# The first expert as 128 early rows and 88 on halves of the array, the second in a fixed third place with its weights loaded in the attention

## The chip, the core and the metric

One core of one Trainium2 chip. The metric is the device time of one execution in microseconds (us); smaller is better. The engines are PE (matmuls; weight loads are recorded apart as PEld), DVE, ACT, POOL and SP. Each takes its instructions in order; SP issues direct transfers, POOL the indirect ones (gathers and scatters by a list of row numbers).

## What is computed

A gated linear recurrence over 4 batches x 8 heads x 768 positions of width 48, and on its output, 3072 tokens of width 384, a mixture of 16 experts chosen in two steps (4 groups of 4). All is float32. Cut to what matters:

```python
for t in range(S):                                   # attention
    state = alpha[:, :, t, :, None] * state + einsum('bhd,bhe->bhde', k[:, :, t], v[:, :, t])
    y[:, :, t] = einsum('bhd,bhde->bhe', q[:, :, t], state)
x = y.transpose(0, 2, 1, 3).reshape(3072, 384)
g = argmax(x @ w_group, 1)                           # mixture
for each group g, expert e (argmax of xg @ w_expert[g]):
    h = maximum(x[tokens] @ w1[g, e], 0)             # 384 -> 1024
    out[tokens] = (g_w * e_w)[:, None] * (h @ w2[g, e])   # 1024 -> 384
```

With the inputs that the reference draws, the experts get 213, 184, 202, 191, 211, 196, 184, 200, 180, 158, 195, 181, 168, 194, 205 and 210 tokens. Of the first 2048 tokens (16 tiles) 131 go to expert 0, of the first 1536 (12 tiles) 96.

## The kernel before, in words

**Attention.** The sequence is cut into 24 chunks (tiles) of 128 tokens, and the recurrence of a chunk is done with matmuls: scores (`scores`, L428), masked, then outputs (`outputs`, L506), what the state adds (`from_before`, L494), the new state (`gains`, L463), and rows and logits (`to_rows`, L527). `outputs` and `gains` write their heads in turn to the lower and upper 64 partitions, so their matmuls use one half of the array's columns at a time. All of this is a list of pieces of work with an engine, a planned duration (`takes`), a time after which others may use the result (`serves`), an action and what it needs; `in_turns` (L35) plans them in order of planned time and due time, and the instructions are emitted in that order, which then is each engine's order. Pieces named below: `OUTn` outputs of chunk n; `LGn` logits; `PAg`, `PBg`, `WTg`, `CNTg`, `PLg` the choice of experts, weights and places for a group g of chunks (L800); `Xt` the scatter of tile t's rows into their expert's slots in `slots_d` (POOL, L625). On SP and on PE the order is that in which the code adds the pieces.

**Slots.** Each expert has slots in DRAM, and a token's place is its number within the expert. `fill` writes blanks first. Inputs q, k and alpha are loaded into buffers that are at the same time the two buffers of expert weights (`homes`, L304; the pool of `w1`, `w2` has two buffers each): a unit's input sits in the first weight buffer when (u + 1) % 3 is 0, in the second when it is 1. Unit 8 is the last in the first, unit 9 the last in the second.

**Early rows.** The first expert's first 96 slots (`EARLY`) are full once the first 12 tiles (`EARLY_T`) are scattered. `LW` (L792) loads its weights into the first buffer when unit 8 has left it, `ER` (L793) reads the 96 rows when `X11` has landed, `ET` turns them on DVE (L649), and the end of the attention on PE is interleaved with their hidden layer: `E0` to `E3`, each two f-blocks (`early`, L875), with relus `A0` to `A3` on ACT, then `RP` (L953), two thirds of their result. The last third (L1189) follows after the attention's PSUM pools have given way to a pool of 7 banks (L969).

**Mixture.** `jobs` (L1131): job 0 the 96 early rows of expert 0, job 1 its slots 96 to 223, then 15 jobs, the other experts in order of their number of tokens, each rank with a fixed number of rows `cap(r)` (L154): 216, 213, ... 180, then 171 and 168. `by_number` (L1097, DVE) sorts; SP reads each job's expert from the result. Per job: `fetch_rows` (SP, up to three jobs ahead), `columns` (DVE transposes of 32x32), `hidden` (24 matmuls and 4 relus), `result` (24 matmuls and 2 copies), `deliver_quarters` (DVE, then one indirect scatter per 32 rows on POOL). Rows are the moving operand; the weights, 128x128 at a time, are loaded for each matmul. The weights of job j + 2 are loaded once job j has left its buffer (L1200); those of job 2 are loaded after its rows are fetched (L1193). Tokens beyond a job's rows would be done in a loop at the end whose number of turns is read from the data.

The two parts that do the matmuls, as they are before:

```python
nc.tensor.matmul(z[:, k * n:(k + 1) * n], lhsT=w1[:, dc, f * P:(f + 1) * P],
                 rhs=xt[:, dc, 0:n], start=(dc == 0), stop=(dc == DC - 1))
```

## Time and profile before

| | |
|---|---|
| median of three runs | 397.62 us (394.83 to 399.1) |
| the profiled execution | 390.5 us |
| its span | 388.8 us, TensorE clock granted 0.992 |
| PE busy | 374.7 us, 96% of the span, 3366 instructions |
| weight loads busy | 356.6 us, 92% |
| POOL, DVE, ACT busy | 195.3, 162.4, 139.3 us |
| DMA | 95.22 MB, mean 245 GB/s |
| first matmul of job 1, of job 2 | 129.73, 141.47 us |

How to read it: the page gives each engine's busy time, the span in 40 slices (9.72 us each) with the DMA rate in each, the chain of work that ended last, followed back from the end, and groups of instructions. The timeline lists instructions in order of start, runs of the same kind merged into one line, with the idle time before and what ended it. An f32 matmul is two instructions in these counts.

### The profile page before, as it was taken

The page shows a single profiled execution, that of the slowest core. Times are in us where ns is not written, and L with a number is a line of the kernel's source. Part 1 is how long each engine was busy: PE and PEld are TensorE (multiplying, and loading weights), DVE is VectorE, ACT ScalarE, POOL GpSimd, SP SyncE. Part 2 cuts the span into 40 slices and gives each one's busy share as a digit, 9 for nine tenths or more (in the row PEclk, how much of TensorE's full clock was granted, in tenths as well). Part 3 has the DMA queues.
Part 4 walks back from the last instruction along what each step waited for, and adds up shares of the span by engine and source line. Part 5 has one row for each costly group of instructions (what it writes and reads, how often), then busy time and mean ns, then how long its engine had stood idle before and what let it go on. Part 6 is the DMA issues. An engine that isn't in the chain of part 4 may idle for free.

```text
span 388.8 us, 8864 instructions
## 1 busy us (share of the span) xinstructions
PE 374.7 (96%) x3366; PEld 356.6 (92%) x3366; DVE 162.4 (42%) x420; ACT 139.3 (36%) x379; POOL 195.3 (50%) x240
## 2 busy tenths in 40 slices
PE   8999999999999899999999999999999999999990
PEld 3888998898989899999999999999999999999990
DVE  7999998899868220207322020220201202202200
ACT  5989899596762211111121121211212112112110
POOL 5988886888746321244261633526336235144341
PEclk9999999999999999999999999999999999999996
DMA  8999999994313799986585866768668777665000
GB/s 284 380 410 412 413 358 352 410 417 172 100 64 128 154 328 346 333 244 219 175 255 218 276 220 207 224 227 282 227 201 257 269 245 240 249 250 182 16 22 27
DMA packets 32411, 95.22 MB, mean 245 GB/s; under 512 B 18175, under 2 KB 18454, under 8 KB 27888
## 3 DMA queue, kind: packets, MB, share of 16 engines
q1 hardware_dynamic: 27552, 85.10, 63.5%
q0 software_dynamic: 4816, 9.55, 7.3%
q8 instruction: 27, 0.44, 0.5%
q14 instruction: 16, 0.13, 0.1%
HBM read 79.47 MB, written 15.56 MB: 244 GB/s over the span
## 4 chain that ended last, share of the span: by engine, by line
PE 69%; DMA 18%; issue 5%; POOL 4%; SPq 1%; DVE 1%; POOLq 0%; ACT 0%; DVEq 0%; ACTq 0%
PE bank L237 29%; PE bank L248 29%; DMA slots_d<-blank 7%; DMA qka<-in_qka_dram 5%; DMA w<-in_qka_dram 3%; PE zo L506 3%; PE zs L428 3%; PE bank L527 2%; DMA out_dram<-yq,dst_q 2%; POOL out_dram L1023 1%; DMA v<-in_v_dram 1%; PE zo L494 1%; SPq L320 1%; POOL slots_d L625 1%; PE bank L446 1%
## 5 line engine op out<-in xcount | busy, mean ns | idle before, releaser
L1023 POOL DMA_INDIRECT out_dram<-yq,dst_q x99 | 96.4, 974 | 153.2 <-DVE yq L1019 121.3
L237 PE MATMUL bank<-xt_e,w 128*128 128x128 f32 (+15 forms) x768 | 126.5, 325 | 1.4 <-DVE dst_q L1045 0.8
L248 PE MATMUL bank<-hT,w 128*128 128x128 f32 (+15 forms) x768 | 126.3, 324 | 0.0
L237 PEld LDWEIGHTS bank<-xt_e,w 128*128 128x128 f32 x768 | 124.1, 190 | 1.7 <-PE bank L248 0.9
L248 PEld LDWEIGHTS bank<-hT,w 128*128 128x128 f32 x768 | 124.1, 190 | 0.0
L1040 DVE CAST dst_q<-xq 128x7 int32<-128x7 f32 (+2 forms) x16 | 2.7, 168 | 168.8 <-DMA out_dram<-yq,dst_q 168.8
L239 ACT ACTIVATE hT<-bank 128x256 f32<-128x256 f32 (+15 forms) x64 | 31.3, 489 | 96.3 <-PE bank L237 96.3
L250 ACT COPY yT<-bank 128x256 f32<-128x256 f32 (+31 forms) x32 | 12.7, 398 | 109.0 <-PE bank L248 109.0
L625 POOL DMA_INDIRECT slots_d<-xr,place x24 | 24.1, 1002 | 10.6 <-issue 3.3
L506 PE MATMUL zo<-sm,v 128*48 128x128 f32 (+1 forms) x384 | 27.2, 280 | 1.0 <-POOL sm L437 1.0
L428 PE MATMUL zs<-qp,kp 48*128 48x128 f32 x384 | 28.2, 285 | 0.0
L527 PE MATMUL bank<-wr,yt 112*128 112x116 f32 x192 | 26.1, 279 | 0.5 <-ACT sm L856 0.5
L506 PEld LDWEIGHTS zo<-sm,v 128*48 128x48 f32 (+1 forms) x384 | 20.3, 129 | 6.5 <-POOL sm L437 2.4
L428 PEld LDWEIGHTS zs<-qp,kp 48*128 48x128 f32 x384 | 23.4, 187 | 2.6 <-DVE qp L414 0.8
L527 PEld LDWEIGHTS bank<-wr,yt 112*128 112x128 f32 x192 | 23.3, 191 | 0.9 <-ACT sm L856 0.7
L405 ACT ACTIVATE w<-w,whole 112x128 f32<-112x128 f32 x60 | 19.8, 402 | 2.0 <-DMA w<-in_qka_dram 2.0
L378 DVE TENSOR_TENSOR_SCAN rev<-w,starts 112x387 f32<-112x387 f32 (+1 forms) x22 | 18.5, 869 | 3.4 <-DMA w<-in_qka_dram 3.4
L414 POOL TENSOR_TENSOR kp<-w,rev 112x384 f32<-112x384 f32 (+1 forms) x21 | 18.3, 886 | 2.2 <-DVE rev L378 2.0
L414 POOL TENSOR_TENSOR qp<-w,cq 112x384 f32<-112x384 f32 (+1 forms) x20 | 17.1, 862 | 4.4 <-ACT w L405 3.9
L433 DVE TENSOR_TENSOR sm<-zs,causal 128x512 f32<-128x512 f32 x28 | 18.3, 679 | 2.4 <-PE zs L428 2.2
L388 DVE TENSOR_TENSOR_SCAN cq<-w,starts 112x387 f32<-112x387 f32 (+1 forms) x22 | 19.1, 871 | 0.0
L1016 DVE STREAM_TRANSPOSE yq<-yT 128x672 f32<-128x672 f32 (+2 forms) x15 | 12.3, 818 | 15.5 <-ACT yT L250 15.4
(135 smaller groups left out, 340.6 us busy)
## 6 DMA issues: line engine op xcount, KB each, us to landing
w<-in_w_dram SPq DMA_DIRECT2D x32, 1536.0 KB, 7.1
w<-in_qka_dram SPq DMA_DIRECT2D x16, 578.0 KB, 10.4
slots_d<-blank SPq DMA_DIRECT2D x4, 1372.0 KB, 19.1
qka<-in_qka_dram SPq DMA_DIRECT2D x8, 578.0 KB, 12.7
v<-in_v_dram SPq DMA_DIRECT2D x3, 1152.0 KB, 15.8
xq<-slots_d SPq DMA_DIRECT2D x32, 85.8 KB, 7.6
qka<-in_qka_dram SPq DMA_DIRECT2D x6, 385.5 KB, 6.3
xq<-slots_d SPq DMA_DIRECT2D x28, 73.5 KB, 6.3
```

The source lines that it names most:

```text
L237: nc.tensor.matmul(z[:, k * n:(k + 1) * n], lhsT=w1[:, dc, f * P:(f + 1) * P], rhs=xt[:, dc, 0:n], start=(dc == 0), stop=(dc == DC - 1))
L239: return lambda: nc.scalar.activation(out=hT[:, f0:f0 + 2, 0:n], in_=z[:, 0:2 * n].rearrange("p (f t) -> p f t", f=2), func=AF.Relu)
L248: nc.tensor.matmul(z[:, i * n:(i + 1) * n], lhsT=w2[:, f, dc * P:(dc + 1) * P], rhs=hT[:, f, 0:n], start=(f == 0), stop=(f == FC - 1))
L378: nc.vector.tensor_tensor_scan(out=part_of("rev", u, i, A1).rearrange("r c s -> r (c s)")[:, ::-1], data0=a[:, W:0:-1], data1=one_col.to_b ...
L388: nc.vector.tensor_tensor_scan(out=cq, data0=a[:, 0:n * A1], data1=starts[0:R, 0:n * A1], initial=1.0, op0=ALU.mult, op1=ALU.min)
L405: nc.scalar.activation(out=q[:, j, :], in_=q[:, j, :], func=AF.Copy, scale=ready["whole", u][:, i * g + j // k, c:c + 1])
L414: engine.tensor_tensor(out=part_of(kind, u, i, P), in0=of, in1=by[:, :, 1:A1], op=ALU.mult)
L428: nc.tensor.matmul(z[i][:, p, :], lhsT=kp[r, p, c, :], rhs=qp[r, p, c, :], start=True, stop=True)
L506: nc.tensor.matmul(of(z, p)[o], lhsT=vs[b][:, bc, h * D:h * D + o.stop - o.start], rhs=sm[:, i, p, :], start=(p < 2 and bc == 0), stop=Tru ...
L527: nc.tensor.matmul(z[:, at:at + W], lhsT=yt[:, p, :], rhs=wr[:, p, :], start=(p == 0), stop=(p % 2 == 1), skip_group_check=True)
L625: dma = nc.gpsimd.indirect_dma_start(out=slots_by[cs.start + c], out_offset=bass.IndirectOffsetOnAxis(ap=it["to"][:, c:c + 1], axis=0), in ...
L1023: nc.gpsimd.indirect_dma_start(out=out_by.popleft().rearrange("n (j w) -> (n j) w", j=4), out_offset=bass.IndirectOffsetOnAxis(ap=dst[:, b ...
```

## The change

What it does, part by part:

- The early rows become 128, read after tile 15 (`EARLY_T` = 16); no group of tiles ends at 16, so the step that raises the count (L614) is no longer reached. All three thirds of their result are in `RP`, in one bank; the last third after the attention is gone.
- Job 1 is the remaining 88 slots of the first expert, which now has 216 in all. Where a job has fewer than 128 rows, `sides` gives two halves, and each 128x128 product is done as two of 64 columns, written to the lower and upper 64 partitions of the same bank, one after the other.
- The second expert is job 2, with 188 rows (`FIXED_CAPS`), whatever its number of tokens. The ranks are 14: 216, 213, ... 183, then 174 and 171.
- Its weights are loaded by `LX`, in SP's order behind `ER`, into the second buffer, when unit 9 has left it. The load at the start of the mixture is gone, and the sort is emitted before the fetch of job 3's rows, not job 2's.
- `blank`, which also holds the early rows' hidden layer, grows to 1024 columns.

```diff
--- before.py
+++ after.py
@@ -148,7 +148,8 @@
     G = Eg = 4
     NL = G + NE
     CAP = 224
-    FIXED, EARLY, EARLY_T, BLK = 1, 96, (B // 2) * NC, 112
+    FIXED, EARLY, EARLY_T, BLK = 2, P, (B // 2) * NC + 4, 112
+    FIXED_CAPS = [CAP - 8, CAP - 36]
     NS = NE - FIXED
 
     def cap(r):
@@ -159,6 +160,7 @@
     XW = 4 * QW
     NB = CAP // 32
     heads = [slice(0, D), slice(64, 64 + D)]
+    halves = [slice(0, 64), slice(64, P)]
 
     cp = ctx.enter_context(tc.tile_pool(name="consts", bufs=1))
     wp = ctx.enter_context(tc.tile_pool(name="weights", bufs=2))
@@ -207,7 +209,7 @@
     wr = cp.tile([R, HP, D2 + NL], F32, name="wr")
 
     picked = cp.tile([P, NT, NE], BF16, name="picked")
-    blank = cp.tile([P, 2 * XW], F32, name="blank")
+    blank = cp.tile([P, max(2 * XW, FC * EARLY)], F32, name="blank")
     seen = cp.tile([P, NT + 1, NE], F32, name="seen")
 
     xr = cp.tile([P, NT, XW], F32, name="xr")
@@ -230,23 +232,31 @@
         weights[i] = (w1, w2)
         return dma.ins
 
-    def hidden_part(z, w1, xt, hT, f0, n, halves=(0, 1)):
-        for k in halves:
-            f = f0 + k
+    def sides(n):
+
+        return [slice(0, P)] if n >= P else halves
+
+    def hidden_part(z, w1, xt, hT, f0, n, of=(0, 1)):
+        for k in of:
+            at = (f0 + k) * P
             for dc in range(DC):
-                nc.tensor.matmul(z[:, k * n:(k + 1) * n], lhsT=w1[:, dc, f * P:(f + 1) * P],
-                                 rhs=xt[:, dc, 0:n], start=(dc == 0), stop=(dc == DC - 1))
+                for x in sides(n):
+                    nc.tensor.matmul(z[x, k * n:(k + 1) * n],
+                                     lhsT=w1[:, dc, at + x.start:at + x.stop],
+                                     rhs=xt[:, dc, 0:n], start=(dc == 0), stop=(dc == DC - 1))
         return lambda: nc.scalar.activation(
             out=hT[:, f0:f0 + 2, 0:n], in_=z[:, 0:2 * n].rearrange("p (f t) -> p f t", f=2),
             func=AF.Relu)
 
-    def result_part(z, w2, hT, yT, d0, n):
-        k = min(2, DC - d0)
+    def result_part(z, w2, hT, yT, d0, n, k=2):
+        k = min(k, DC - d0)
         for i in range(k):
-            dc = d0 + i
+            at = (d0 + i) * P
             for f in range(FC):
-                nc.tensor.matmul(z[:, i * n:(i + 1) * n], lhsT=w2[:, f, dc * P:(dc + 1) * P],
-                                 rhs=hT[:, f, 0:n], start=(f == 0), stop=(f == FC - 1))
+                for x in sides(n):
+                    nc.tensor.matmul(z[x, i * n:(i + 1) * n],
+                                     lhsT=w2[:, f, at + x.start:at + x.stop],
+                                     rhs=hT[:, f, 0:n], start=(f == 0), stop=(f == FC - 1))
         return lambda: nc.scalar.copy(out=yT[:, d0:d0 + k, 0:n],
                                       in_=z[:, 0:k * n].rearrange("p (c t) -> p c t", c=k))
 
@@ -289,7 +299,7 @@
         for t in state:
             nc.scalar.copy(out=t.rearrange("r p e -> r (p e)"),
                            in_=zeros[0:R, 0:1].to_broadcast([R, HP * 64]))
-        nc.scalar.copy(out=blank, in_=zeros[:, 0:1].to_broadcast([P, 2 * XW]))
+        nc.scalar.copy(out=blank[:, 0:2 * XW], in_=zeros[:, 0:1].to_broadcast([P, 2 * XW]))
         nc.scalar.copy(out=quarters[:, :, :, QW - 1], in_=quarter_f)
 
         NU = len(units)
@@ -611,7 +621,7 @@
                 old, new = seen[:, cs.start, :], seen[:, cs.stop, :]
                 nc.vector.tensor_tensor(out=new, in0=rk[:, C, :], in1=old, op=ALU.add)
                 if cs.stop == EARLY_T:
-                    nc.vector.tensor_scalar(out=new[:, 0:FIXED], in0=new[:, 0:FIXED],
+                    nc.vector.tensor_scalar(out=new[:, 0:1], in0=new[:, 0:1],
                                             scalar1=float(EARLY), scalar2=None, op0=ALU.max)
                 rk = rk[:, 0:C]
                 nc.vector.tensor_tensor(out=rk, in0=rk, in1=old[:, None, :]
@@ -654,7 +664,7 @@
             in_turn(
                 out=slots_d.rearrange("(e n) w -> e n w", e=NE)[e:e + n, 0:CAP, :].rearrange(
                     "e (p t) w -> p e (t w)", t=2),
-                in_=blank[0:CAP // 2, None, :].to_broadcast([CAP // 2, n, 2 * XW]))
+                in_=blank[0:CAP // 2, None, 0:2 * XW].to_broadcast([CAP // 2, n, 2 * XW]))
 
         later = {}
 
@@ -664,8 +674,8 @@
             later["desc_f"] = iota("desc_f", [P, 4], [[-1, 4]], base=4)
             nc.gpsimd.iota(out=seen[:, 0, :], pattern=[[N, NE]], base=0, channel_multiplier=0,
                            allow_small_or_imprecise_dtypes=True)
-            nc.gpsimd.memset(blank.rearrange("p (k w) -> p k w", w=QW)[:, :, QW - 1:QW],
-                             float(4 * N))
+            nc.gpsimd.memset(blank[:, 0:2 * XW].rearrange("p (k w) -> p k w", w=QW)
+                             [:, :, QW - 1:QW], float(4 * N))
 
 
 
@@ -791,6 +801,8 @@
         lent = max(u for u in range(NU) if (u + 1) % 3 == 0)
         queued("LW", 7.5, 9.5, lambda: load_weights(0, 0, in_turn), each("KP", lent) + each("QP", lent))
         queued("ER", 2.0, 5.0, read_early, [f"X{EARLY_T - 1}"])
+        lent = max(u for u in range(NU) if (u + 1) % 3 == 1)
+        queued("LX", 7.5, 9.5, lambda: load_weights(2, 1, in_turn), each("KP", lent) + each("QP", lent))
         add("CONST", POOL, 0.6, 0.7, constants, each("QP", 0))
         add("DESC", DVE, 0.13, 0.25,
              lambda: nc.vector.tensor_copy(out=desc, in_=later["desc_f"]), ["CONST"])
@@ -950,10 +962,10 @@
                 count(g)
         early(2)
         early(3)
-        on_array("RP", 3.0, 3.2, lambda: hold.update(RP=result_part(
-            bank(), weights[0][1], early_hT, early_xt, 0, EARLY)), ["A0", "A1", "A2", ("A3", 0.6)],
-            readers=["AR"])
-        add("AR", ACT, 0.4, 0.55, lambda: hold["RP"](), ["RP"])
+        on_array("RP", 5.2, 5.4, lambda: hold.update(RP=result_part(
+            bank(), weights[0][1], early_hT, early_xt, 0, EARLY, DC)),
+            ["A0", "A1", "A2", ("A3", 0.6)], readers=["AR"])
+        add("AR", ACT, 0.5, 0.65, lambda: hold["RP"](), ["RP"])
 
         all_ = {name: Work(e, takes, serves, emit, (), due)
                 for name, (e, takes, serves, emit, _, _, due) in works.items()}
@@ -1116,7 +1128,8 @@
         with nc.allow_low_precision("whole numbers below 2**24"):
             nc.vector.tensor_reduce(out=order, in_=sq, axis=AX.X, op=ALU.add)
         excess, ceiling = (rp.tile([P, NE], F32, name=k) for k in ("excess", "ceiling"))
-        nc.vector.memset(ceiling[:, 0:FIXED], float(CAP))
+        for e, n in enumerate(FIXED_CAPS):
+            nc.vector.memset(ceiling[:, e:e + 1], float(n))
         nc.vector.tensor_scalar(out=ceiling[:, FIXED:NE], in0=rank, scalar1=float(cap(1) - cap(0)),
                                 scalar2=float(cap(0)), op0=ALU.mult, op1=ALU.add)
         drop = cap(1) - cap(0) + cap(NS - 3) - cap(NS - 2)
@@ -1128,7 +1141,8 @@
         nc.vector.tensor_tensor(out=ceiling, in0=ceiling, in1=seen[:, 0, :], op=ALU.add)
         return order, excess, ceiling
 
-    jobs = [dict(e=0, n=EARLY, rows=early_rows), dict(e=0, c0=EARLY, n=CAP - EARLY)]
+    jobs = [dict(e=0, n=EARLY, rows=early_rows), dict(e=0, c0=EARLY, n=FIXED_CAPS[0] - EARLY),
+            dict(e=1, c0=0, n=FIXED_CAPS[1])]
     jobs += [dict(r=r, c0=0, n=cap(r)) for r in range(NS)]
     for job in jobs:
         job["nb"] = -(-job["n"] // 32)
@@ -1176,23 +1190,17 @@
     AHEAD = 3
     for j, job in enumerate(jobs):
         for k in range(1 if j == 0 else j + AHEAD, j + AHEAD + 1):
-            if k == 2:
+            if k == 3:
                 order, excess, ceiling = by_number()
             if k < len(jobs):
-                dma = fetch_rows(jobs[k])
-                if k == 2:
-                    fetched = dma.ins.name
+                fetch_rows(jobs[k])
         width = job["n"]
-        w1, w2 = weights[0] if j < 2 * FIXED else weights.pop(j)
+        w1, w2 = weights[0] if j < 2 else weights.pop(j)
         dst = destined(job)
         if j == 0:
-            result_part(bank(), w2, early_hT, early_xt, 2, EARLY)()
             last = (job, early_xt, dst)
             for t in results:
                 nc.gpsimd.memset(t, 0.0)
-            tc.add_manual_dep(load_weights(2, expert(jobs[2])), fetched, mybir.DependencyInfo(
-                mybir.DependencyClass.NoSync, mybir.DependencyReason.SCHED_ONLY),
-                reason="the rows go ahead of the weights")
             xt = columns(jobs[1])
             continue
         hT = hidden(w1, xt, width, {2: [deliver_last]})
```

## The prediction

> **What bounds the kernel.** I read the page first: PE is busy 96% of the span, and the chain that ended last is PE for 69%.
>
> ```profile
> PE 69%; DMA 18%; issue 5%; POOL 4%; SPq 1%; DVE 1%; POOLq 0%; ACT 0%; DVEq 0%; ACTq 0%
> ```
>
> Then the chain in order of time (start, length, what). From 141.47 us it is matmuls alone, job after job; its last two lines are the job with 171 rows:
>
> ```profile
> 350.74 6.96 PE bank L237 x48
> 357.70 6.97 PE bank L248 x48
> ```
>
> A job is 48 matmuls; an f32 matmul is two instructions, hence 96. 13.93 us / 96 = 145 ns, which is (171 + 3) / 1.2. The same holds for 180 rows (7.32 + 7.32 us) and 213 (8.64 + 8.64). So a job of n rows costs 0.08 us x (n + 3), and one row more anywhere costs 0.08 us.
>
> Next PE's timeline where attention hands over (start, length, operation, shapes, instructions, idle before and releaser):
>
> ```profile
> 116.19 0.91 PE L237 MATMUL zs<-early_xt,w 128*128 128x96 f32 x6
> 116.94 0.18 PE L601 MATMUL bank<-picked,before 128*128 128x32 bf16 x1
> 120.21 2.90 PE L237 MATMUL bank<-early_xt,w 128*128 128x96 f32 x24
> 122.95 3.74 PE L248 MATMUL bank<-blank,w 128*128 128x96 f32 x32
> 127.09 2.02 PE L248 MATMUL bank<-blank,w 128*128 128x96 f32 x16 [0.41 <-ACT early_xt L250]
> 129.73 5.62 PE L237 MATMUL bank<-xt_e,w 128*128 128x128 f32 x48 [0.61 <-DVE dst_q L1040]
> 135.19 5.52 PE L248 MATMUL bank<-hT,w 128*128 128x128 f32 x48
> 141.47 0.79 PE L237 MATMUL bank<-xt_e,w 128*128 128x216 f32 x3 [0.76 <-DVE dst_q L1045]
> ```
>
> The reader is to see two things. With 96 rows, 24 instructions take 122.95 - 120.21 = 2.74 us, 114 ns each; with 128 rows, 48 take 135.19 - 129.73 = 5.46 us, 114 ns each. So 96 and 128 rows cost the same: a floor holds both, about 11.0 us a job. And PE idles only 0.41, 0.61 and 0.76 us. The last idle time is put down to dst_q, but the matmul reads only xt_e, which was done at 132.84, and the weights; these were issued at 132.41 (SP's timeline below), so they end this wait.
>
> The same timeline has matmuls on halves of the columns. Outputs (L506: 64 or 48 columns, 128 moving rows) and gains (L463: 64 or 48 columns, 48 rows) alternate sides:
>
> ```profile
> 110.84 1.09 PE L506 MATMUL zo<-sm,v 128*48 128x128 f32 x16
> 111.75 0.64 PE L463 MATMUL bank<-v,kt 128*48 128x48 f32 x16
> 112.31 1.16 PE L428 MATMUL zs<-qp,kp 48*128 48x128 f32 x16
> ```
>
> From start to start 16 instructions take 0.91 us (57 ns) and 0.56 us (35 ns). On the whole array 131 / 1.2 = 109 ns each would be needed for L506, so two halves run at once.
>
> Last, the queues and DVE around the early rows:
>
> ```profile
> 98.11 1.01 POOL L625 DMA_INDIRECT slots_d<-xr,place  x1 [0.15 <-DVE starts L591]
> 106.46 0.97 POOL L625 DMA_INDIRECT slots_d<-xr,place  x1 [1.79 <-DVE lg L533]
> 100.93 2.73 SPq L320 DMA_DIRECT2D early_rows<-slots_d  x4
> 132.41 0.35 SPq L226 DMA_DIRECT2D w<-in_w_dram  x1
> 106.21 0.47 DVE L649 STREAM_TRANSPOSE early_xt<-early_rows 128x288 f32<-128x288 f32 x1
> 115.08 0.19 DVE L533 TENSOR_REDUCE lg<-bank 128x20 f32<-128x40 f32 x1
> 116.67 0.19 DVE L577 TENSOR_TENSOR picked<-oh,starts 128x32 bf16<-128x32 f32 x1
> ```
>
> Counting scatters back from the last (X23, 122.46), 98.11 is X11 and 106.46 is X15. The early rows' transposition began 8.1 us after X11's start.
>
> **What the Trainium skill says.** TensorE: Matmul & The Clock Gate, section LDWEIGHTS: a weight load takes its columns / 1.2 ns, 106.7 for 128. The trace agrees: loads of 128, 64 and 48 columns last 190, 137 and 123 ns, 0.83 ns a column, and the floor of 114 ns is 107 plus some. The same page, Part 3, says that loads overlap matmuls in flight only when the row group differs, which halves of columns do not. TensorEngine Tiling (Array Packing), Key Properties, says that different tiles load and multiply in parallel, and that changing the mode drains the engine. L463 sides with the second page: its 16 loads, 896 columns, would take 0.75 us one after the other and took 0.56. The drain has no row of its own. DMA: Bandwidth & Descriptors, Queues, rings and completion order: each DMA engine takes turns between queues by packet, so a weight load beside scatters slows them; no moment here shows late scatters beside a weight load.
>
> **The change part by part.** Times are against the profiled execution (390.5 us, span 388.8, so 1.7 outside); the median of the runs, 397.62, lies 1.8% higher, and I carry the difference over unscaled.
>
> *Early part, 96 to 128 rows.* At the floor: 0. All 48 matmuls now stand in the attention, so the 0.41 us before the last third (its bank came from the next pool, after ACT's copy) goes: -0.41; the wait for that pool meets job 1 instead, 0.5 to 0.6 us (one ACT copy) under the wait for its rows. ACT's relus grow from 0.33 to 0.39 us (the 128x256 rows), under 1.34 us of matmuls each. The reference's inputs give expert 0 131 tokens in the first 16 tiles, so all 128 slots are filled.
>
> *ER waits for X15 in place of X11.* 8.1 us after X15 is 114.6. Behind ER in SP's line stand only the new load and the rows of the later jobs, due at 125. In DVE's order the transposition falls where the planner expects its data (1.5 + 5.0 us after X15), in the middle of routing, about the logits at 115.08. There it costs DVE 0.58 us (128x384, the duration of job 1's), and what follows on DVE, picked at 116.67 first, is late by about 0.5 us; PE waits for picked at 116.94, having 0.08 us to spare: +0.45 for PE, and as much for X23 and job 1's rows. Bounds: 0 (a place in DVE's idle 0.7 to 1.9 us at 112) and +1.5 (data a microsecond late too).
>
> *LX, the second expert's weights in the attention.* Two transfers of 1536 KB behind ER, from 112; at 390 to 410 GB/s (slices 3 to 6 of the page) 3.15 MB take 8 us, done by 120, where slices 11 to 13 show 64 to 128 GB/s used. X23 leaves POOL at 123. So 0, with 0 to +1 if it delays the last scatters. Its target is unit 9's buffer, last read at 87. In return job 2 doesn't wait for weights: -0.76. Job 3's weights go out after job 1's hidden part, near 134, and are needed 18 us later; a load lands in 7.1.
>
> *Job 1 starts* at the later of PE (129.1 + 0.6) and its rows (129.67 + 0.45 - 0.12 for a transposition of three blocks, not four, = 130.0): +0.25.
>
> *Job 1, 128 whole to 88 on halves.* 192 instructions. Best: the stream alone, 96 pairs x (88 + 3) / 1.2 = 7.3 us. L506 stands 4% above its stream (114 against 109 a pair): 7.6 us. A straight line between L463 and L506 at 88 rows gives 46 ns each, 8.8. No gain (loads one after the other, 57 each): 11.0. I take 7.6: -3.4. ACT's four relus, 0.33 us each, come every 0.95.
>
> *More rows.* Before, ranks 216, 213, ... 180, 171, 168 sum to 2913; after, 188 and 14 ranks sum to 2927: 14 x 0.08 = +1.12. Nothing is left over in either: expert 0 has 213 tokens for 216, expert 1 184 for 188, and the other counts lie under their ranks.
>
> *Switching halves on and off*: +0.1 to 0.3; the 0.24 us by which job 2's first phase (9.00) exceeds its second (8.76) goes: 0 together. Sort of 14 for 15, rows of job 2 without the sort's register: off the path (DVE idles 3.44 us before 129.09).
>
> Sum: 0.25 - 3.4 - 0.76 + 1.12 = **-2.8 us**; span 386.0, profiled 387.7, median 394.8.
>
> **Rivals.** *Halves win little*: the first page's rule on row groups holds and pairs go at 57 ns or near. For: L506's 57 ns would look the same. Against: L463. Sum -0.9 to +0.6. *Slower*: at L237 and L248 each half instruction costs a whole array's 114 ns, because the halves drain each other: job 1 becomes 22 us, +11.0, total about +8.2 (+2%); it turns slower once an instruction costs over 72 ns (192 x 72 = 13.8 us). Against: L506 and L463. *Early rows late*: LX's packets hold up ER or the scatters, and DVE stands at the transposition with the routing behind it. If ER landed with LX at 120, all shifts by 4.8: +2.0. Against: ER is issued ahead. *More than I count*: the whole handover closes up, the transposition finds idle time, the halves at 7.1: -4.4. That expert 1 overflows, each block then costing a turn of the last loop, the counts exclude.
>
> **How the numbers follow.** Forecast 0.62, its own range -3.8 to -1.5; little from halves 0.16, slower 0.07, early rows late 0.08, more 0.07. 1% (4.0 us) is about what a measurement here can tell from no change, since three runs spread by 4.3 us; that spread also blurs the forecast of -0.7%, of which a good third falls beyond the bound. Faster 0.35, within 0.52, slower 0.13 (the slower rival, and a late early part with more behind it). Range: -4.4 and 2 us of spread below give 391.2, +1.0 above 398.6.
>
> **What would show it.** L237 and L248 of 88 rows near 40 ns an instruction; job 1 from about 130.0 to 137.6; job 2 with no idle time before it; early_xt's transposition near 115 with no DVE wait; PE's last matmul 2.8 us earlier. Wrong if halves cost 57 ns or more, or if DVE waits for the early rows.

## The result, and the profile after

The changed kernel takes 402.23 us at the median of 21 runs (399.08 to 405.3), the kernel before beside it 396.82 us (394.25 to 399.44): ratio 1.0127, 95% interval 1.0098 to 1.0157. It is slower by 1.3%, where 394.8 us and a range of 391.2 to 398.6 were forecast.

The profiled execution of the changed kernel took 402.47 us, span 400.7, TensorE clock granted 0.978; the one before had a span of 388.8. On the page PE is still the bound:

```profile
PE 79%; issue 6%; DMA 4%; POOL 4%; DVE 2%; SPq 1%; ACT 0%; POOLq 0%; ACTq 0%
```

PE's timeline at the handover, for comparison with the one shown of before (start, length, operation, shapes, instructions, idle before and releaser):

```profile
127.45 5.60 PE L257 MATMUL bank<-blank,w 128*128 128x128 f32 x48 [1.42 <-DVE key L1116]
134.53 3.37 PE L244 MATMUL bank<-xt_e,w 128*64 128x88 f32 x82 [1.48 <-ACT early_xt L260]
138.10 0.40 PE L244 MATMUL bank<-xt_e,w 128*64 128x88 f32 x4 [0.20 <-issue]
138.85 0.35 PE L244 MATMUL bank<-xt_e,w 128*64 128x88 f32 x3 [0.34 <-issue]
...
141.76 0.39 PE L244 MATMUL bank<-xt_e,w 128*64 128x88 f32 x1 [1.13 <-issue]
141.77 6.76 PE L257 MATMUL bank<-hT,w 128*64 128x88 f32 x96
148.47 1.70 PE L244 MATMUL bank<-xt_e,w 128*128 128x188 f32 x9
```

Job 1 starts at 134.53 instead of 129.73. Its first 82 instructions take 41 ns each (3.37 us / 82), near the forecast; then PE issues a few at a time with nothing that the program makes it wait for ("issue"), for some 4 us. I call such a stretch a **stand**. The result layer takes 70 ns an instruction instead of 40: the granted clock was halved from 140.88 to 147.71 us. And the end of the chain of waits (start, length, what):

```profile
358.41 7.08 PE bank L244 x48
365.50 7.09 PE bank L257 x48
...
382.20 5.76 issue
389.56 1.55 POOL out_dram L1020
```

The last delivery's scatter on POOL holds this chain for 1.55 us. In the kernel before it takes 0.94 us (POOL's timeline):

```profile
381.31 0.94 POOL L1008 DMA_INDIRECT out_dram<-yo,dst_m  x1 [0.30 <-issue]
```

Cut into four pieces by such times, the spans differ like this:

| | before | after | |
|---|---|---|---|
| first matmul of job 1 | 129.73 | 134.53 | +4.8 |
| job 1, to job 2's first matmul | 11.74 | 13.94 | +2.2 |
| job 2 to the end of PE's last matmul | 238.0 | 239.1 | +1.1 |
| from there to the end of the span | 9.4 | 13.1 | +3.7 |

This is +11.8, twice what the medians differ by (5.4). The experiments give a reason: the profiled execution of before (390.5 us) was one without stands, and its other runs (394 to 399 us) were, by their times, with them.

### The profile page after: what moved, and what is told of

Its sections match the earlier page's. It is cut to its first block, busy times and chain, and to the rows that moved or that the text cites. A ratio compares the mean times of both kernels' runs of the same rounds, so it can differ in the third digit from the quotient of the medians.

```text
span 400.7 us, 9046 instructions
## 1 busy us (share of the span) xinstructions
PE 376.5 (94%) x3462; PEld 357.8 (89%) x3462; DVE 162.8 (41%) x422; ACT 138.7 (35%) x378; POOL 195.5 (49%) x240
## 4 chain that ended last, share of the span: by engine, by line
PE 79%; issue 6%; DMA 4%; POOL 4%; DVE 2%; SPq 1%; ACT 0%; POOLq 0%; ACTq 0%
PE bank L257 31%; PE bank L244 30%; PE zs L438 5%; PE zo L516 4%; DMA w<-in_qka_dram 4%; PE bank L537 4%; PE zo L504 2%; PE bank L456 2%; PE bank L473 2%; SPq L330 1%; POOL out_dram L1035 1%; POOL qp L424 1%; POOL sm L447 1%; POOL slots_d L635 1%; POOL out_dram L1020 1%
## 5 line engine op out<-in xcount | busy, mean ns | idle before, releaser
L244 PE MATMUL bank<-xt_e,w 128*64 128x88 f32 (+15 forms) x816 | 126.7, 319 | 3.9 <-issue 2.4
L257 PE MATMUL bank<-hT,w 128*64 128x88 f32 (+15 forms) x816 | 128.1, 329 | 0.0
L244 PEld LDWEIGHTS bank<-xt_e,w 128*128 128x128 f32 (+1 forms) x816 | 123.4, 184 | 5.0 <-issue 3.2
L257 PEld LDWEIGHTS bank<-hT,w 128*128 128x128 f32 (+1 forms) x816 | 125.9, 193 | 0.0
L247 ACT ACTIVATE hT<-bank 128x176 f32<-128x176 f32 (+15 forms) x64 | 31.1, 485 | 98.9 <-PE bank L244 73.6
L260 ACT COPY yT<-bank 128x176 f32<-128x176 f32 (+31 forms) x32 | 12.6, 395 | 110.7 <-PE bank L257 110.7
L635 POOL DMA_INDIRECT slots_d<-xr,place x24 | 24.0, 999 | 14.2 <-issue 7.5
L1028 DVE STREAM_TRANSPOSE yq<-yT 128x672 f32<-128x672 f32 (+2 forms) x15 | 12.2, 811 | 23.9 <-ACT yT L260 23.8
```

The costliest lines, as they stand in the source:

```text
L244: nc.tensor.matmul(z[x, k * n:(k + 1) * n], lhsT=w1[:, dc, at + x.start:at + x.stop], rhs=xt[:, dc, 0:n], start=(dc == 0), stop=(dc == DC ...
L247: return lambda: nc.scalar.activation(out=hT[:, f0:f0 + 2, 0:n], in_=z[:, 0:2 * n].rearrange("p (f t) -> p f t", f=2), func=AF.Relu)
L257: nc.tensor.matmul(z[x, i * n:(i + 1) * n], lhsT=w2[:, f, at + x.start:at + x.stop], rhs=hT[:, f, 0:n], start=(f == 0), stop=(f == FC - 1))
L635: dma = nc.gpsimd.indirect_dma_start(out=slots_by[cs.start + c], out_offset=bass.IndirectOffsetOnAxis(ap=it["to"][:, c:c + 1], axis=0), in ...
```

## The experiments

Theory A at the outset: load and halves make TensorE stand, and the stands are the loss. Rival B: the stands come by chance, in either kernel, and the loss is elsewhere. The times of the kernel before changed from one set of runs to the next (389.6, 399.9, 396.2, 389.3, 399.75 us at the median); only ratios to it in the same set are compared.

**Both kernels once more** (no edit).

> The kernel before once more, for its profile. The changed kernel's profile shows PE standing still three times with nothing in the program to wait for: at about 102.5 to 104.3, 121 to 125 and 137.7 to 141.8 us. Theory A (the second expert's load, in flight at 112 to 125, and the halves bring them about): none here; first matmul of job 1 near 129.7, of job 2 near 141.5, span near 389. Theory B (such pauses are chance and fall into every execution): one or more pauses of over 1 us on PE here too, at other places, and a span of 392 to 398.

> The changed kernel once more, for its profile. Theory A: the pauses come back at the same places, X23 near 128 and job 2's first matmul near 148. Theory B: they fall elsewhere or are missing; without any, X23 near 123.5, job 1 from about 130 and job 2 from about 138, span near 387.

One run each: 388.37 and 393.86 us, the kernel before 389.6 at the median. Neither has a stand. So the changed kernel is slower without stands too, and A is not enough. Job 1 still started 1.8 us later than in the kernel before, after 2.56 us of idle time, and the end took 13.1 us after the last matmul against 9.0.

**Whole columns, and the load at its old place.** The first edit takes the halves out, the second puts the second expert's weights back behind the rows.

```diff
-        return [slice(0, P)] if n >= P else halves
+        return [slice(0, P)]
```
```diff
-        queued("LX", 7.5, 9.5, lambda: load_weights(2, 1, in_turn), each("KP", lent) + each("QP", lent))
...
+            tc.add_manual_dep(load_weights(2, 1), fetched, ...)
```

> The changed kernel with job 1's 88 rows on the whole array. If the halves are what costs (job 1 took 13.9 us with them, with a pause from 137.7 and a lower clock after it), job 1 takes 11.0 us and the kernel is about 3 us faster than the changed one: ratio to the kernel before near 1.005. If the halves save what was forecast (7.6 for 11.0) and the load is to blame, it is about 3 us slower than the changed kernel: ratio near 1.02.

> The changed kernel with the second expert's weights loaded where the kernel before loads them, behind the rows of jobs 1 to 3. If the load beside the last scatters is the cause, X23 comes back from 127.9 to about 123 us, job 1 starts near 130, job 2 waits for its weights until about 141, and the ratio to the kernel before is near 1.00. If not, job 2 waits for its weights and the rest stays: ratio 1.013 or more.

Whole columns: ratio 1.0402 (1.0334 to 1.0470). PE's timeline, then the stretches of 5 us (bounds; length, busy time of PE, PEld, DVE, ACT, POOL; granted clock; DMA share, GB/s):

```profile
131.21 10.52 PE L244 MATMUL bank<-xt_e,w 128*128 128x88 f32 x48 [2.84 <-issue]
141.52 10.45 PE L257 MATMUL bank<-hT,w 128*128 128x88 f32 x48
```
```profile
125.00:130.00 5.00, 3.37 (x31) 3.18 (x29) 0.45 (x4) 0.48 (x1) 0.00 (x0) 1.00 0.28 76
135.00:140.00 5.00, 5.00 (x25) 5.00 (x25) 0.27 (x3) 0.64 (x2) 1.97 (x3) 0.50 0.46 109
145.00:150.00 5.00, 5.00 (x25) 5.00 (x25) 0.00 (x0) 0.31 (x1) 0.00 (x0) 0.50 0.43 177
```

Job 1 takes 20.6 us, nearly twice 10.8, because the granted clock fell to 0.50 at the end of the idle time and stayed there for 23.9 us, all of job 1 long. Neither expectation had this.

Late load: ratio 1.0192 (1.0126 to 1.0257). PE:

```profile
128.29 3.86 PE L244 MATMUL bank<-xt_e,w 128*64 128x88 f32 x96 [0.57 <-ACT early_xt L260]
131.98 3.81 PE L257 MATMUL bank<-hT,w 128*64 128x88 f32 x96
140.89 10.08 PE L244 MATMUL bank<-xt_e,w 128*128 128x188 f32 x48 [5.10 <-DMA w<-in_w_dram]
```

This is the forecast's job 1: it starts at 128.3 and takes 7.5 us, 39.1 ns an instruction (7.50 / 192). But the shorter job leaves the load less cover: job 2 waits 5.10 us for the weights, and the clock is halved for 6.8 us, from within that wait on, so that its hidden layer takes 10.08 us instead of 7.9. With the long end, told below, still in it, this kernel takes 397.17 us at the median of four runs, the changed one 393.86 in its one run: the old place of the load is the dearer one.

So the load, where it now is, costs job 1's start. How, the trace of the changed kernel in a later execution shows (its run is told below), beside that of the kernel before. POOL's and SP's timelines of the kernel before:

```profile
121.95 0.97 POOL L625 DMA_INDIRECT slots_d<-xr,place  x1 [0.93 <-ACT blank L239]
124.75 7.93 SPq L1150 DMA_DIRECT2D xq<-slots_d  x12
```

and of the changed kernel, with the line of DVE that waits for the rows:

```profile
112.96 0.88 SPq L330 DMA_DIRECT2D w<-in_w_dram  x2
123.34 0.97 POOL L635 DMA_INDIRECT slots_d<-xr,place  x1 [1.25 <-ACT blank L247]
128.62 6.86 SPq L1164 DMA_DIRECT2D xq<-slots_d  x11
131.93 0.48 DVE L1043 STREAM_TRANSPOSE xt_e<-xq 128x288 f32<-128x288 f32 x1 [5.39 <-DMA xq<-slots_d]
```

The DMA issues from 110 to 128 us, with the median time to landing in us, in the kernel before:

```profile
slots_d<-xr,place POOLq DMA_INDIRECT x8, 2.9
```

and in the changed kernel:

```profile
w<-in_w_dram SPq DMA_DIRECT2D x2, 1536.0 KB
slots_d<-xr,place POOLq DMA_INDIRECT x8, 7.2
```

The scatters land in 7.2 us instead of 2.9 (of the eight, the trace has the landing of two here and of one there). X23 begins at 123.34, the last packet of the weights ends at 125.87, and the fetch of job 1's rows, which waits for X23, goes out at 128.62. Over all the profiles: with no weights in flight the fetch comes 2.7 to 2.8 us after X23's start (the kernel before, late load, early load), and as soon where they had landed before it. Where X23 starts before the weights have landed it comes 4.8 to 5.8 us after X23, and 2.6 to 3.0 us after the weights' last packet (six profiles; in a seventh the weights landed 0.2 us after X23's start, and it comes 3.3 us after that). The last scatter is in effect served when the weights have landed. The Trainium skill, DMA: Bandwidth & Descriptors, Queues, rings and completion order, has each DMA engine take turns between the queues by packet. The traces agree: from 118 to 123 us 121 packets of the scatters' queue went out beside 151 of the weights' queue, where the kernel before had 234; from 126 to 128 us, with the weights through, 107 did.

**The end.** The packets after PE's last matmul, in the kernel before:

```profile
DMA packets 113, 0.26 MB, mean 21 GB/s; under 512 B 41, under 2 KB 68, under 8 KB 112
```

and those of the changed kernel:

```profile
DMA packets 402, 0.27 MB, mean 16 GB/s; under 512 B 336, under 2 KB 353, under 8 KB 400
```

About as many bytes, but 336 packets below 512 bytes (288 of them of 12 bytes) instead of 41. The last job has 171 rows instead of 168, so its two deliveries have 112 and 59 rows instead of 112 and 56. Two edits, one on each kernel:

```diff
-            for t, n in enumerate((BLK, job["n"] - BLK)):
+            for t, n in enumerate((BLK, 64)):
```
```diff
-    FIXED, EARLY, EARLY_T, BLK = 1, 96, (B // 2) * NC, 112
+    FIXED, EARLY, EARLY_T, BLK = 1, 96, (B // 2) * NC, 109
```

> The changed kernel with one edit: the second of its two last deliveries takes 64 partitions instead of 59 (the five added rows carry the place of an unused slot and are dropped). In the changed kernel's second profile this delivery of 59 rows held POOL for 1.65 us and its last packet ended 6.1 us after its issue, with 288 packets of 12 bytes among them; in the kernel before the 56-row delivery held POOL for 0.95 us and ended 2.0 us after its issue. Theory T (a count of 59 rows is cut up badly): POOL holds it for 0.95 us, it ends 2.0 to 2.5 us after its issue, the span ends 6.1 us instead of 9.5 after the last tensor work, and the kernel comes 3 to 3.5 us nearer to the one before: ratio 1.0127 - 0.0085, about 1.004. Rival U (the dropped rows cost, of which there are now 18 instead of 13, or the tail is chance): the delivery takes as long as with 59 rows or longer, ratio 1.012 or more.

> The kernel before with one edit: its last deliveries of 112 and 56 rows become 109 and 59. Nothing else of the change is in it. Theory T: the 59-row delivery alone brings the long tail: it holds POOL for 1.65 us, ends 6 us after its issue, and the kernel is 3 to 4 us slower than before (ratio 1.008 to 1.010; more if the 109 rows are cut up in the same way). Rival U: ratio 1.000 to 1.002, since the number of dropped rows stays 10.

With 64 rows: ratio 0.9997 (0.9968 to 1.0025), and in two later sets 1.0032 (1.0000 to 1.0063) and 0.9994 (0.9962 to 1.0025). The kernel before with 109 and 59 rows: 1.0194 (1.0148 to 1.0239), more than T's 1.008 to 1.010, since the 109 rows are cut up too. Packets at the end, with 64 rows and then with 109 and 59 (the last line is its deliveries on POOL: shortest, median and longest, in ns):

```profile
DMA packets 115, 0.28 MB, mean 21 GB/s; under 512 B 41, under 2 KB 64, under 8 KB 112
```
```profile
DMA packets 945, 0.27 MB, mean 13 GB/s; under 512 B 890, under 2 KB 892, under 8 KB 944
...
L1008 POOL DMA_INDIRECT out_dram<-yo,dst_m x2: 1649/1988/2327, 389.4 to 392.1; - x2
```

From PE's last matmul to the end of the span: 9.0 to 9.8 us in all profiles with 112 and 56 or 64 rows, 13.1 in all five with 112 and 59, 17.9 with 109 and 59. (The 9.5 and 6.1 us of the expectations count from the end of POOL's last scatter instead.) Theory T is shown, on both kernels; U, which blamed the dropped rows, falls, as 64 rows drop five more.

**The load earlier, and TensorE kept busy.** In both the last delivery has 64 rows.

```diff
-        queued("ER", 2.0, 5.0, read_early, [f"X{EARLY_T - 1}"])
         lent = max(u for u in range(NU) if (u + 1) % 3 == 1)
         queued("LX", 7.5, 9.5, lambda: load_weights(2, 1, in_turn), each("KP", lent) + each("QP", lent))
+        queued("ER", 2.0, 5.0, read_early, [f"X{EARLY_T - 1}"])
```
```diff
             xt = columns(jobs[1])
+            z = bank()
+            for _ in range(20):
+                nc.tensor.matmul(z[:, 0:P], lhsT=ident, rhs=ident, start=True, stop=True)
             continue
```

> The last delivery of 64 rows, and the second expert's weights issued ahead of the early rows in SP's order, so that they land well before the last scatters. Theory L (the weights in flight beside the last scatters are what made the rows of job 1 late): the first fetch of job 1 is issued 2.7 us after X23 starts, as with the late load, and not 4.8; job 1 starts at 128.3 to 129, TensorE waits under 1 us for it, the clock is not halved, job 1 takes 7.5 us, job 2 starts at 136.5 without a wait, and the span is 3 us shorter than that of the kernel with the 64-row delivery alone: ratio about 0.996. Rival M (the scatters are late for another reason, or the early rows behind 3 MB of weights come late): the fetch still comes 4.5 us or more after X23, job 1 at 130 or later, ratio 1.004.

> The last delivery of 64 rows, and 20 matmuls of 128x128 (about 2.3 us) that compute nothing used, between the third third of job 0 and job 1, where TensorE stood 2.56 us in the changed kernel's second profile. Theory C (the clock is halved because TensorE stands there): no halved stretch near 130, the hidden layer of job 1 takes 3.7 us instead of 5.4, and the span is 1.5 us shorter than with the 64-row delivery alone. Rival D (the clock falls for another reason, such as the change from whole columns to halves or the power of the program as a whole): a halved stretch of 3.4 us or more stays in job 1, and the time is the same or up to 0.5 us longer.

Ratios 1.0010 (0.9984 to 1.0037) and 1.0001 (0.9966 to 1.0037): no gain from either. But in this set the kernel before took 399.9 us, and all the profiles have stands near 103 us. They delay X23 to 126.5 in the kernel with 64 rows alone, past the weights' landing at 126.3: its fetch came 2.73 us after X23, with nothing for an earlier load to win. As for the clock, no stretch of it was halved at the handover of the busy kernel, as C has it; but none was in the kernel with 64 rows alone either, where TensorE idled only 1.31 us (its clock was halved later, at 140.4, in job 1's stand). So C and D were not put to the test. The 20 matmuls took 4.7 us, twice my estimate (they are 40 instructions), and delayed job 1 from 133.19 to 137.45; job 1 then took 9.44 us instead of 12.95, with a shorter stand and a full clock, and the one made up for the other.

PE's timeline of the kernel with 64 rows, in job 1:

```profile
133.19 3.29 PE L244 MATMUL bank<-xt_e,w 128*64 128x88 f32 x81 [1.31 <-ACT early_xt L260]
136.82 0.32 PE L244 MATMUL bank<-xt_e,w 128*64 128x88 f32 x2 [0.34 <-issue]
...
140.49 0.72 PE L244 MATMUL bank<-xt_e,w 128*64 128x88 f32 x6 [1.13 <-issue]
...
146.15 7.91 PE L244 MATMUL bank<-xt_e,w 128*128 128x188 f32 x48
```

Again the stand comes after some 80 instructions. Job 1 takes 12.95 us, longer than on whole columns in the kernel before.

**Whose are the stands?** Next to each other: the kernel before; with 64 rows; with 64 rows and whole columns (the first edit above); with 64 rows and the early load.

> The kernel before, once more, beside the next three. It took 389.6 us at the median beside the first experiments and 399.9 us beside the second ones, and its two profiles so far (390.5 and 388.4 us) have no stretch in which TensorE stands still without a wait that the program holds; the kernels of the second experiments have such stretches near 103, 122 and 138 us. Theory B (these stretches come with the place where a kernel runs and not with the change): where the time is 395 us or more, this kernel's profile has them too, some 5 to 9 us of them between 100 and 130 us, and where it is near 389 neither this one nor the next three has. Rival A (they belong to the changed kernel): none in this one, whatever its time.

> The changed kernel with the last delivery of 64 rows, once more, as the base for the next two. Beside the second experiments its ratio was 0.9997. Without standing stretches: the first fetch of job 1 4.8 us after the last scatter starts, TensorE idle 2.5 us before job 1, a halved stretch of 3.4 us in job 1, and 3.4 us less than the changed kernel's second profile (393.9): 390.4, ratio 1.002 to a kernel before of 389.6. With them: as before, 0.9997.

> The last delivery of 64 rows, and job 1's 88 rows on whole columns, the halves left out. Prediction's theory (the halves save 3.4 us of job 1): 3.4 us slower than the base at full clock. What the first experiments showed (88 rows on whole columns keep the clock halved for 24 us, once it is): 12 us slower, ratio 1.030. Rival H (where TensorE stands still in job 1, it is the halves that bring it, and they cost what they save): 0 to 2 us slower or faster than the base, no standing stretch in job 1's hidden layer, which takes 5.5 us as the kernel before's does.

> The last delivery of 64 rows, and the second expert's weights ahead of the early rows, once more. Beside the second experiments this gave nothing (ratio 1.001), where the last tile's scatter started at 126 to 128 us, after the late weights had landed at 126.3. Theory L (weights in flight beside the last scatter cost 2 us): where the last scatter of the base starts before its weights have landed (122 to 124 us), the fetch comes 2.7 us after the scatter instead of 4.8, job 1 starts 2 us earlier, the clock is not halved, and this kernel is 3 to 3.7 us faster than the base: ratio 0.993. Where it starts after that: no gain, 0 to +0.5 us.

The kernel before took 395.7 us, and now has stands itself (PE's timeline):

```profile
102.53 0.86 PE L428 MATMUL zs<-qp,kp 48*128 48x128 f32 x4
103.73 0.52 PE L428 MATMUL zs<-qp,kp 48*128 48x128 f32 x5 [0.33 <-issue]
104.47 0.59 PE L428 MATMUL zs<-qp,kp 48*128 48x128 f32 x5 [0.22 <-issue]
105.22 0.48 PE L428 MATMUL zs<-qp,kp 48*128 48x128 f32 x2 [0.16 <-issue]
```

The same scores, in an execution without, run through in one line, 16 in 1.16 us. Theory B holds: the stands in the attention belong to the execution, not to the change. They cost more than their gaps: the clock was halved for 6.8 us from 105.6 on, and job 1 starts at 137.78 instead of 128.93. That in job 1 is another matter. The ratios are 1.0032 on halves and 1.0023 (0.9994 to 1.0051) on whole columns; job 1 takes 13.1 us on halves, with the stand and 6.8 us of halved clock, and 11.8 on whole columns, with a full clock:

```profile
133.72 5.56 PE L244 MATMUL bank<-xt_e,w 128*128 128x88 f32 x48 [1.47 <-ACT early_xt L260]
139.12 1.50 PE L257 MATMUL bank<-hT,w 128*128 128x88 f32 x12
141.44 4.25 PE L257 MATMUL bank<-hT,w 128*128 128x88 f32 x36 [0.81 <-ACT hT L247]
```

The hidden layer takes 5.56 us, without a stand (the result layer has one gap, put down to ACT); rival H holds. In all eight profiles of job 1 on halves in which TensorE stands in the attention it stands in job 1 too, and the halves lose there what they win elsewhere. The early load: 1.0019 (0.9986 to 1.0052).

**The changed kernel again, and one layer at a time.** All but the first with 64 rows. Only the result, then only the hidden layer, on halves; then 50 more matmuls at the start of PE's stream.

```diff
-                for x in sides(n):
+                for x in [slice(0, P)]:
                     nc.tensor.matmul(z[x, k * n:(k + 1) * n],
```
```diff
-                for x in sides(n):
+                for x in [slice(0, P)]:
                     nc.tensor.matmul(z[x, i * n:(i + 1) * n],
```
```diff
-        of_ones(14)
+        for _ in range(64):
+            nc.tensor.matmul(idle[:, 0:64], lhsT=ones, rhs=ones[:, 0:64], start=True, stop=True)
```

> The changed kernel as it is, beside the next three. Theory T (the 59-row delivery costs 3.4 us and more): ratio to the kernel before 1.012 to 1.014, as at first, and the span ends 9.5 us after the last tensor work. Rival: with the last delivery of 64 rows the ratio was 1.000 to 1.003 only because of the place where it ran; then this one too comes to 1.004 or less there.

> The last delivery of 64 rows; job 1's hidden layer on whole columns and only its result layer on halves. Theory Q (TensorE stands because halves issue 52 instructions per us where whole columns issue 18, after some 160 of them): the hidden layer takes 5.5 us without a stand, and the stand appears in the result layer, after about 80 of its 96 matmuls or in its last gap, so job 1 takes 12 to 13 us. Rival V (the stand belongs to the place in time or in the stream where the hidden layer runs): the result layer takes 3.8 us, job 1 takes 9.3 to 9.5 us, and the kernel is 1.5 to 2.5 us faster than the one with both layers on whole columns (1.0023 there): ratio about 0.998.

> The last delivery of 64 rows; only job 1's hidden layer on halves, its result layer on whole columns. Theory Q and rival V alike expect the stand in the hidden layer where the kernel before takes 395 us or more (7.5 to 8 us instead of 3.7), and 5.5 us for the result layer at full clock: job 1 13.2 us, ratio 1.005. Where the kernel before takes 389 us: 3.7 us and 5.5 us, job 1 9.2 us.

> The last delivery of 64 rows, and 50 more matmuls (100 instructions) at the very start, where TensorE waits for its first data; it may start up to 1 us later. All that follows stands 100 instructions later in TensorE's stream. Theory position (the stand comes at a fixed place of the stream, where a new block of instructions begins): it moves 50 matmuls ahead in the hidden layer, to after 30 of its 96, instead of after 80. Theory Q (so many dense instructions after the last wait): it stays after 80 of the 96.

The kernel before took 389.3 us here, and none of the four stands in job 1; so the question of the stand's place could not be answered. The rest could. The changed kernel: 1.0146 (1.0056 to 1.0235). Its PE timeline is the cleanest of all:

```profile
123.85 5.52 PE L257 MATMUL bank<-blank,w 128*128 128x128 f32 x48
132.50 3.86 PE L244 MATMUL bank<-xt_e,w 128*64 128x88 f32 x96 [3.13 <-issue]
136.17 3.84 PE L257 MATMUL bank<-hT,w 128*64 128x88 f32 x96
139.94 7.91 PE L244 MATMUL bank<-xt_e,w 128*128 128x188 f32 x48
```

PE idles 3.13 us before job 1, until DVE has turned the rows (its line is shown above), and job 1 then takes 7.43 us. Only the hidden layer on halves: 1.0083 (1.0058 to 1.0109), job 1 10.9 us with 3.4 us at half the clock. Only the result: 1.0173 (1.0110 to 1.0236), job 1 15.8 us, with the clock halved for 13.7 us from early in its whole-column hidden layer on. The shifted stream: 391.65 us in one run.

**The early load, beside its base.** The same two kernels once more, for an execution without stands.

> The changed kernel with the last delivery of 64 rows, as the base of the next one. If TensorE does not stand between 100 and 125 us (kernel before near 389): the last scatter starts at 122 to 124 us, the first fetch of job 1 5 us after it, TensorE idle 2.5 to 3.5 us before job 1, job 1 7.4 us, or 9 where the clock halves; the last delivery lands as in the kernel before; 389.5 to 391 us, ratio 1.001 to 1.005. If it does stand (kernel before 395 or more): ratio 1.000 to 1.003, as before.

> As the base, with the second expert's weights ahead of the early rows. If TensorE does not stand between 100 and 125 us: theory L: first fetch 2.7 us after the last scatter, job 1 at 128.3 to 129.3 with under 1 us of idle before it, no halved clock, job 1 7.5 us, job 2 without a wait at 136.5; 2.5 to 4 us faster than the base and 2 to 3 us faster than the kernel before, ratio 0.993. Rival M (the rows are late for another reason, or the early rows behind 3 MB of weights make job 0 late): 0 to 1 us faster than the base. If it does stand: no gain, 1.001 to 1.002 as before.

It didn't come: the kernel before took 399.75 us. Ratios 0.9994 (0.9962 to 1.0025) and 1.0051 (1.0027 to 1.0074). So no kernel here beats the one before; what the early load is worth where X23 and the weights do meet was not seen, and theory L rests on the late load and on the comparison of the profiles.

## Why the prediction was wrong

The changed kernel in its third profile (393.82 us, job 1 at 132.50) and the kernel before in its second (388.37 us) both have no stand, and both have a full clock in job 1; they ran on different chips. The kernel before, in PE's timeline:

```profile
128.93 5.62 PE L237 MATMUL bank<-xt_e,w 128*128 128x128 f32 x48 [0.32 <-DVE dst_q L1040]
139.75 8.95 PE L237 MATMUL bank<-xt_e,w 128*128 128x216 f32 x48
```

Their difference, by the prediction's own steps:

| step | forecast | measured |
|---|---|---|
| job 1's start | +0.25 | +3.6 (128.93 to 132.50) |
| job 1 on halves | -3.4 | -3.4 (10.82 to 7.43) |
| job 2's wait for weights | -0.76 | gone, but 0 in this profile of before |
| 14 more rows | +1.12 | +1.2 on PE |
| the end, after PE | no step for it | +4.1 (8.96 to 13.08) |
| span | -2.8 | +5.5 (386.6 to 392.1) |

*Two steps failed, and a third where TensorE stands.* The first is the term **"LX ... So 0, with 0 to +1 if it delays the last scatters"**. The prediction had the weights done by 120 and X23 leaving POOL at 123. In the profiles without stands they were issued at 111 to 114, landed at 124 to 126.5, and held the last scatters back by 2 to 3 us, two to three times the bound. 3.15 MB in 12.9 us (112.96 to 125.87) is 244 GB/s; the 400 that I took came from slices (410, 412, 413 and 358 GB/s, not quite the 390 to 410 that it says) that end before the first scatter, at 69 us. In the +3.6, 2.5 us are the fetch's lag behind X23 (5.28 for 2.80); 1.4 us that X23 itself started later, against 0.45 forecast; -0.3 the shorter fetch. Between the two second profiles, of one set and one chip, the start moves by 1.8: 2.0 of lag, 0.2 of X23, -0.4 of the fetch. The second is **"More rows ... 14 x 0.08 = +1.12"**: right for PE, but the ranks also set the shape of the last delivery, and 59 rows were never priced. That costs +3.7 to +4.1 after everything else has ended, with no cover, and alone turns the forecast's sign.

In the set of the result itself, whose profile has stands, the first step cost nothing that shows: the weights had landed at 127.16 when X23 began at 127.88, and the fetch came 2.74 us after it. There the third step failed, **"I take 7.6: -3.4"**. Beside the kernel before in its profile with stands (span 396.0, from another set) the changed kernel's first profile reaches job 2 at the same time, 148.47 against 148.60: job 1 starts 3.2 us earlier but takes 13.94 us, not 10.82. The 14 rows then add 1.2 us and the end 3.6, together +4.7 on the span, where the medians differ by 5.4.

*Right.* Job 1 on halves: 38.7 ns an instruction (7.43 / 192) against a forecast of 39.6 (7.6 / 192). The slower rival (halves that drain each other) and that of little gain fall: no half instruction took 57 ns at full clock without a stand. The rival of late early rows had the right culprit, LX's packets, and named the scatters, but it priced a late landing of the early rows, where it was X23 that came late. The early rows' transposition on DVE made PE wait 0.35 us for `picked` in the second profile (and not at all in the third) where 0.45 was forecast. The 0.41 us of idle time before job 0's last third went, but job 1's wait for its rows swallowed it. Two figures of the slower rival are off: its +8.2 takes away a gain that it rules out (0.25 + 11.0 - 0.76 + 1.12 = +11.6), and for the same reason the change turns slower from 54 ns an instruction on (10.4 us for job 1), not from 72.

*Not in the prediction.* Where 2.3 to 4.0 us passed from the last matmul's start to job 1's, the clock was halved in six profiles of seven; after 2.2 us, in the kernel before, it was not. At half the clock the halves' gain falls (job 1 9.0 us, in two profiles), so the late start is paid for twice. And where TensorE stands, job 1 on halves takes 12.9 to 14.2 us in all profiles but two (11.1, and 9.4 behind the added matmuls), and these two are the ones whose clock was not halved in job 1. What a stand is stays open: the trace shows matmuls issued a few at a time with no wait, in the same few places of either kernel, at times on the chip where there had been none before. One trait stands in the traces, and no run tests it: in all eleven profiles with a stand near 103 us it begins 1.0 to 2.2 us after a packet of 16 KB on the queue that the page calls "instruction" has started, and that in job 1 begins 1.1 to 3.8 us after a later one has. In the other profiles the same packets pass without a stand. That TensorE waits there for its instructions is a rival that nothing here excludes.

The Trainium skill's page TensorE: Matmul & The Clock Gate says that loads overlap matmuls in flight only across row groups (Part 3); TensorEngine Tiling (Array Packing), Key Properties, lets different tiles load and multiply in parallel. The second one is what 38.7 ns an instruction bears out: at the 0.83 ns a column that the prediction read from the trace of before, a load of 64 columns would by itself take 53 ns (an estimate: 64 x 0.83).

## What to carry to other kernels

A changed number of rows changes more than the matmuls: price each transfer whose shape it sets, the last one above all, because nothing covers it. A load put into an idle-looking stretch was free here only where it had landed before the last small transfer that someone waits for was issued; take its rate from a stretch with that same traffic. And an idle time ahead of a short job costs more than its length where the clock falls.

## What the hardware showed that was not expected

- Indirect scatters of 112, 56 and 64 rows of 1536 bytes went out in packets of mostly 1536 to 4608 bytes; 59 and 109 rows added 288 and more packets of 12 bytes. The 59 rows held POOL for 1.65 us instead of 0.93 to 0.96, and their last packet ended 6.1 us after the issue instead of 2.0 to 2.6.
- A clock once halved came back after 3.4 or 6.8 us with halves or long jobs following, but stayed halved for 13.7 us through one layer, and 23.9 us through two, of 88 rows on whole columns with PE busy throughout. The halved stretches last 3.41, 6.83, 13.65 and 23.89 us: 1, 2, 4 and 7 times 3.41.
- The kernel before itself took 389.3 and 389.6 us at the median of two sets and 396.2 to 399.9 in four others; its profile from one of the longer ones, 397.69 us, has stands in the attention, and on one chip both were seen at different times.
